# Where the sums of the first-layer weights are built, and in which form the second layer of the first sweep runs

## The chip, the core and the metric

The kernel runs on one core of a Trainium2 chip. The metric is the device time of one execution in microseconds (us), the median of several runs. Engines are named as in the profile: PE is TensorE (PEld its weight loads), DVE is VectorE, ACT is ScalarE, POOL is GpSimd, SP is SyncE, which in this kernel issues every DMA.

## What is computed

A causal, windowed attention (8 batches, 8 heads, 576 positions, head dimension 64, window 128, a linear bias by distance) gives 4608 tokens of 512 features. Two matrix products with a piecewise function between them follow. All is float32.

```python
rel = pos[:, None] - pos[None, :]
mask = (rel >= 0) & (rel < window)
scores = np.where(mask, scale * q @ k.T + bias, -1e9)
x = (softmax(scores) @ v)                      # 4608 x 512 after the heads are put side by side
h = x @ w_in                                   # 512 -> 2048
g = np.where(h >= 1, h, np.where(h <= -1, 0.0, (h + 1) ** 2 / 4))
out = g @ w_out                                # 2048 -> 512
```

## The kernel before

**Sweeps.** The 4608 tokens are cut into nine chunks of 512. Each chunk has a sweep (number c = 0 to 8) over the eight groups g of the feed-forward part; a group is two blocks of 128 of the 2048 hidden features, fc = g and fc = 8 + g. While the sweep of chunk c runs, the attention of chunk c + 1 is worked between its matmuls. What "first sweep" and "second sweep" mean below is c = 0 and c = 1.

**First layer.** In the first sweep a group is four plain products with the blocks A11, A12, A21, A22 of w_in (`plain`, L838 through `product`). From the second sweep on it is seven products with A11, A12, A22 and four sums of blocks, S1 to S4 (`prod`), in the manner of Strassen and Winograd. A float32 operand is kept as a high part of type float32r and a low part, the rest; a product is then three float32r matmuls of high and low parts. `build` makes such a pair out of a float32 block: a rounding copy (L506, through `rounded`, on ACT or DVE) and a subtraction on DVE (L507), and stores it to DRAM (L510). `operand` makes the sums first, with one DVE addition or subtraction each (L494). Later sweeps load the pairs from DRAM into a ring of ten tiles (`fetch`, L516). In the first sweep both the plain blocks and, once a group's A22 is asked for, its four sums are built.

**Weights.** They arrive as 64-bit numbers, so a block `raw` of 512 KB (L421) is turned into float32 by two passes of ACT (L451, L461) and two of DVE (L456, L464) in `convert`. A float32 first-layer group lies in one of three tiles (`w_of`).

**Second layer.** `layer2` adds the product of g's block with a block of w_out to four accumulators in PSUM, one per 128 tokens. Mostly both are high and low parts and there are three float32r matmuls (L879 to L881); `nonlinear` makes the parts of g (gh, L859, and gl, L861) and `split_out` those of w_out (L477, L478). In the first sweep groups 0 to 4 (`g < WHOLE`) do without: g and w_out stay float32 (tile `fo`), and one float32 matmul stands for the three (L872). For these groups `split_out` is called in the second sweep, where the parts are first needed.

**Slots.** `raw`, `fo` and the split w_out blocks `wo` share 17 slots of 4 KB per partition ("w" in pool "wp", NW = 17). 16 of them are in the end held by the 16 `wo`, for the rest of the kernel.

**Order.** `Plan` sets the order: every operation is recorded with its engine or engines, a cost, and what it reads and writes. A list scheduler with due times then lays them out (it may move a rounding copy, or the first step of `nonlinear`, from ACT to DVE or back), and the instructions are emitted in that order. On the chip each engine runs its own list strictly in that order.

Of the kernel before, what the change touches and what calls it, by code (L numbers as in the profile page):

```python
# [56 lines left out]
class Plan:  # L57
# [22 lines left out]
    def op(self, alts, reads=(), writes=()):  # L80

        node = Node(alts, set())
        reads = [x if isinstance(x, tuple) else (x, None) for x in reads]
        writes = [x if isinstance(x, tuple) else (x, None) for x in writes]

        def touched(table, key):
            return [n for k, v in table.items() if key is None or k is None or k == key for n in v]

        for b, key in reads + writes:
            assert not b.over, b.name  # L90
            if b.before is not None:
                b.before.over = True
            node.deps.update(touched(b.writers, key))
        for b, key in writes:
            node.deps.update(touched(b.readers, key))
            if not touched(b.writers, key) and b.before is not None:
                node.deps.update(b.before.nodes)
        for b, key in writes:
            if key is None:
                b.writers, b.readers = {}, {}  # L100
            b.writers[key] = [node]
            b.readers.pop(key, None)
        for b, key in reads:
# [191 lines left out]
def windowed_attention_then_ffn(  # L295
# [26 lines left out]
    LIGHT = 2  # L322
    FIRST = 1
    WHOLE = 5
# [99 lines left out]
    def convert(i):  # L424
# [6 lines left out]
        elif g < WHOLE:  # L431
            if f == 0:
                fo[g] = plan.shared(pools["wp"], "w", NW, [P, 2, DM], F32, f"fo_{g}", lambda free: True)
                kept.append((g, fo[g]))
            w, key = fo[g], f
# [30 lines left out]
    def split_out(g, f):  # L466

        o, key = (fo[g], f) if g < WHOLE else (fo.pop((g, f)), None)
        w = wo_of[f * NG + g] = plan.shared(pools["wp"], "w", NW, [P, 2, DM], F32R, f"wo_{g}_{f}", lambda free: (
            g >= WHOLE or all(x.slot is not None for _, x in kept)))  # L470
        if g >= WHOLE:
            kept.append((g, w))

        def whole():
            return o.t if key is None else o.t[:, key]

        plan.op(rounded(DM, lambda: w.t[:, 0], whole), [(o, key)], [(w, 0)])  # L477
        plan.op(dve(DM, lambda: V.tensor_tensor(w.t[:, 1], whole(), w.t[:, 0].bitcast(F32), ALU.subtract), True),  # L478
                [(o, key), (w, 0)], [(w, 1)])

    scratch, sums_w = {}, {}
# [17 lines left out]
    def build(g, name):  # L499
        b, key, f = operand(g, name)  # L500
        if name in PLAIN:
            t = buf("ring", "r", 10, [P, 2, 2, P], F32R, f"b_{g}_{name}")
        else:
            i = SUMS.index(name)
            t = buf(*(("ap", f"kk{i}", 1) if i < 2 else ("fp", "o", 2)), [P, 2, 2, P], F32R, f"b_{g}_{name}")
# [19 lines left out]
    def load_qk(p):  # L525
# [14 lines left out]
        if c < LIGHT:  # L540
# [10 lines left out]
    def load_v(p):  # L551
# [7 lines left out]
        if c < LIGHT and p % 2:  # L559
# [8 lines left out]
    def prepare_q(p):  # L568
# [5 lines left out]
        elif c < LIGHT:  # L574
# [4 lines left out]
        for j in range(2):  # L579
            if c < LIGHT:  # L580
# [54 lines left out]
    def scores(m, blks):  # L635
# [34 lines left out]
        if c < LIGHT:  # L670
# [26 lines left out]
    def weights_t(m):  # L697
# [13 lines left out]
        if c < LIGHT:  # L711
# [36 lines left out]
    def values(m):  # L748
# [32 lines left out]
        if c < LIGHT:  # L781
# [63 lines left out]
    def nonlinear(c, fc, h, src, f):  # L845
# [18 lines left out]
    def layer2(c, n, fc, t):  # L864
# [5 lines left out]
        if c == 0 and fc % NG < WHOLE:  # L870
            w, g, key = fo[fc % NG], gs[c, fc], fc // NG
            plan.op(pe(0.861, lambda: T.matmul(a.t, g.t[:, ts], w.t[:, key], start=first, stop=False)), [g, (w, key)], [a])  # L872
# [24 lines left out]
    for m in range(NH):  # L897
# [6 lines left out]
        if j and p + 1 < NH // 2:  # L904
# [20 lines left out]
    def weights_upto(n):  # L925
        while converted[0] < min(n, len(WEIGHTS)):
# [4 lines left out]
            if second_matrix and g >= WHOLE:  # L931
# [8 lines left out]
    def operands_upto(n):  # L940
        while asked[0] < min(n, len(todo_w)):
# [19 lines left out]
    def sweep_steps(c):  # L961
        steps = []
        for g in range(NG):
# [36 lines left out]
            def plain(i, tt, st=st, g=g):  # L1000
# [24 lines left out]
            if c == 1 and g < WHOLE:  # L1025
                steps[-1].append(lambda g=g: (split_out(g, 0), split_out(g, 1)))
# [68 lines left out]
```

## Time and profile before

| | |
|---|---|
| runs before | 993.31, 993.52, 994.74 us; median 993.52 us |
| the profiled execution | 994.51 us, of which its span on the core is 992.7 us |
| granted clock of PE | 1.00 in the whole span |
| first sweep's feed-forward (first to last group's start of the next sweep) | about 41 to 161 us |
| second sweep | 161.15 to 267.7 us |
| third sweep | 267.7 to 373.3 us |
| HBM | 176.82 MB read, 26.21 MB written |

A row of a group of instructions reads: line, engine, operation, out<-in by the program's names, shapes, count | busy us, mean ns of one | idle time of the engine ahead of them and what ended it. The busy time of an engine is the union of its instructions' records; two DVE or ACT instructions that follow each other at once overlap in the record by nearly 0.1 us, so the step from start to start is shorter than the mean of one. A row of a wait reads: who waited for whom: us in all, times, longest. A row of windows reads: the stretch, its length, then the busy time of PE, PEld, DVE, ACT, POOL with the count of instructions, the granted clock, the DMA engines' busy share, GB/s.

### The profile page before, as it was taken

Reading aid. Unit: us, or ns where it says so; the run is one execution under the profiler, and the core shown is the slowest. Engines: PE = TensorE matmul, PEld = TensorE weight load, DVE = VectorE, ACT = ScalarE, POOL = GpSimd, SP = SyncE. Lnnn points to the kernel's source line nnn. Section 1 sums busy time; section 2 is a strip of 40 time slices with the busy share of each in tenths; the row PEclk is TensorE's granted clock in tenths of the full one; section 3 lists DMA queues with packets and bytes.
Section 4 is the critical chain, followed back from the end, with each engine's and each line's share of the span. In section 5 each row is a group of like instructions: output and inputs, shape, how many; then the busy total and the mean of one; then the engine's idle time right before and its main releaser. Section 6 shows DMA issues by size and latency. Waiting matters only on the chain.

```text
span 992.7 us, 19604 instructions
## 1 busy us (share of the span) xinstructions
PE 983.4 (99%) x6456; PEld 886.2 (89%) x6456; DVE 813.5 (82%) x2118; ACT 654.5 (66%) x1619; POOL 195.5 (20%) x274
## 2 busy tenths in 40 slices
PE   9999999999999999999999999999999999999998
PEld 8887779989989999999999999999999999998987
DVE  7899999997887789777987798878877897885453
ACT  7997767966776568666775577667765676654222
POOL 3310201221231114111321122112311131210000
PEclk9999999999999999999999999999999999999999
DMA  9778885766676666766576658665766677456651
GB/s 347 296 237 289 301 299 168 243 185 197 177 227 189 188 191 204 222 181 198 174 239 200 189 165 260 185 182 179 244 187 186 188 202 222 154 159 193 188 157 43
DMA packets 104532, 204.33 MB, mean 206 GB/s; under 512 B 12400, under 2 KB 12400, under 8 KB 104432
## 3 DMA queue, kind: packets, MB, share of 16 engines
q1 hardware_dynamic: 104432, 203.08, 66.6%
q8 instruction: 53, 0.87, 0.4%
q14 instruction: 47, 0.39, 0.1%
HBM read 176.82 MB, written 26.21 MB: 205 GB/s over the span
## 4 chain that ended last, share of the span: by engine, by line
PE 92%; ACT 4%; DVE 2%; DMA 1%; issue 1%; POOL 0%; ACTq 0%; DVEq 0%; POOLq 0%
PE hA L838 17%; PE hB L838 13%; PE acc L879 12%; PE acc L880 12%; PE acc L881 12%; PE x L775 8%; PE h L838 5%; PE acc L872 3%; PE p L708 3%; PE s L668 3%; PE s L667 2%; ACT z L681 1%; PE s L665 1%; DMA out_dram<-o 1%; PE idle L1032 0%
## 5 line engine op out<-in xcount | busy, mean ns | idle before, releaser
L879 PE MATMUL acc<-wo,gh 128*128 128x512 f32 x536 | 216.5, 404 | 0.0
L880 PE MATMUL acc<-wo,gh 128*128 128x512 f32 x536 | 211.8, 395 | 0.0
L881 PE MATMUL acc<-wo,gl 128*128 128x512 f32 x536 | 210.1, 392 | 0.0
L739 POOL TENSOR_SCALAR_AFFINE_SELECT lu<-lu 128x512 fp32r<-128x512 f32 x112 | 92.9, 829 | 568.7 <-ACT lu L732 551.7
L982 ACT COPY s<-hA 128x256 f32<-128x256 f32 x192 | 70.7, 368 | 97.8 <-PE hA L838 96.9
L977 DVE TENSOR_TENSOR h<-hB,s 128x256 f32<-128x256 f32 x192 | 80.8, 421 | 54.0 <-PE hB L838 31.3
L681 ACT ACTIVATE z<-z,nmax 128x128 f32<-128x128 f32 x288 | 112.7, 393 | 16.9 <-DVE nmax L677 16.2
L881 PEld LDWEIGHTS acc<-wo,gl 128*128 128x128 f32 x536 | 100.7, 188 | 22.8
L838 PEld LDWEIGHTS hA<-x_T,w_S 128*128 128x128 f32 x768 | 107.3, 189 | 9.8 <-ACT s L982 0.4
L838 PE MATMUL hA<-x_T,w_S 128*128 128x256 f32 x768 | 111.9, 281 | 0.0
L879 PEld LDWEIGHTS acc<-wo,gh 128*128 128x128 f32 x536 | 101.7, 190 | 8.3
L880 PEld LDWEIGHTS acc<-wo,gh 128*128 128x128 f32 x536 | 101.8, 190 | 7.6
L852 ACT ACTIVATE m<-m 128x512 f32<-128x512 f32 x144 | 90.5, 628 | 21.6 <-DVE m L849 19.8
L854 DVE SCALAR_TENSOR_TENSOR h<-h,m 128x512 f32<-128x512 f32 x128 | 88.4, 691 | 9.8 <-ACT m L852 9.5
L861 DVE TENSOR_TENSOR gl<-h,gh 128x512 fp32r<-128x512 f32 x128 | 88.3, 690 | 2.6 <-ACT gh L359 0.7
L674 DVE COPY_PREDICATED s<-older,s 128x256 f32<-128x256 uint32 x144 | 60.6, 424 | 24.7 <-PE s L668 17.9
L742 POOL TENSOR_SCALAR_AFFINE_SELECT lu<-lu 128x512 fp32r<-128x512 f32 x112 | 75.4, 696 | 0.0
L775 PEld LDWEIGHTS x<-lu,vs 128*128 128x128 f32 x560 | 71.2, 190 | 2.6 <-POOL lu L742 0.5
L677 DVE CUSTOM_DVE_ANT_0 z<-s,rel 128x128 f32<-128x128 f32 x288 | 70.9, 285 | 1.6
L775 PE MATMUL x<-lu,vs 128*128 128x256 f32 (+1 forms) x560 | 71.3, 274 | 0.1
L849 DVE TENSOR_SCALAR m<-h 128x512 f32<-128x512 f32 x86 | 38.8, 451 | 37.8 <-ACT h L988 35.1
L988 ACT COPY h<-hA 128x256 f32<-128x256 f32 x64 | 23.8, 371 | 66.5 <-PE hA L838 65.6
(119 smaller groups left out, 2106.7 us busy)
## 6 DMA issues: line engine op xcount, KB each, us to landing
w_S<-d_S SPq DMA_DIRECT2D x256, 256.0 KB, 2.8
w_A<-d_A SPq DMA_DIRECT2D x192, 256.0 KB, 2.9
kr<-in_k_dram SPq DMA_DIRECT2D x112, 160.0 KB, 3.2
vn<-in_v_dram SPq DMA_DIRECT2D x33, 320.0 KB, 3.7
out_dram<-o SPq DMA_DIRECT2D x36, 256.0 KB, 3.9
qr<-in_q_dram SPq DMA_DIRECT2D x33, 256.0 KB, 3.2
raw<-in_moe_w_in_dram SPq DMA_DIRECT2D x16, 512.0 KB, 5.7
raw<-in_moe_w_out_dram SPq DMA_DIRECT2D x16, 512.0 KB, 6.9
```

The lines of the kernel that those rows point to most:

```text
L681: plan.op({"ACT": (0.385, 0.48, lambda i=i: S.activation(z.t[:, i], z.t[:, i], AF.Exp, bias=nmax.t[:, i:i + 1], scale=-1.0, accum_out=sm.t ...
L739: G.affine_select(out=lu[s].t[:, 0:2 * nb:2], in_=a.bitcast(F32), pattern=[[0, nb], [-1, P]], base=0, channel_multiplier=1, compare_op=ALU ...
L742: G.affine_select(out=a, in_=a.bitcast(F32), pattern=[[0, nb], [1, P]], base=0, channel_multiplier=-1, compare_op=ALU.is_ge, fill=0.0)
L775: T.matmul(px[:, q0 * P:q1 * P], sv, mv.rearrange("p a w -> p (a w)"), start=(w == 0), stop=(w == len(todo) - 1), skip_group_check=True)
L838: T.matmul(o.t[:, at:at + 2 * P], w.t[:, a, kb], x.t[:, b, kb], start=start and n == 0, stop=stop and n == len(todo) - 1, skip_group_check ...
L852: plan.op(act_fn(n, lambda: S.activation(m.t, m.t, AF.Square, scale=0.5)), [m], [m])
L854: plan.op(dve(n, lambda: V.scalar_tensor_tensor(f.t, h.t, 1.0, m.t, ALU.max, ALU.min), not psum), src + [m], dst)
L861: plan.op(dve(n, lambda: V.tensor_tensor(gl.t, f.t, gh.t.bitcast(F32), ALU.subtract), True), dst + [gh], [gl])
L879: T.matmul(a.t, gh.t[:, ts], w.t[:, 0], start=first, stop=False)
L880: T.matmul(a.t, gh.t[:, ts], w.t[:, 1], start=False, stop=False)
L881: T.matmul(a.t, gl.t[:, ts], w.t[:, 0], start=False, stop=last)
L977: plan.op(dve(2 * P, lambda: V.tensor_tensor(f.t[:, key * 2 * P:(key + 1) * 2 * P], b.t[:, :2 * P], s.t, ALU.add)), [b, s], [(f, key)])
```

## The change

1. `WHOLE` goes. In the first sweep every group has g and w_out in high and low parts and three float32r matmuls; `split_out` runs for all sixteen blocks in the first sweep, and the float32 matmul of L872 goes.
2. `LATE = 6`: for groups 2 to 7 the sums S1 to S4 are no longer built in the first sweep. `spill` stores the group's float32 first-layer weights to DRAM (two DMAs of 256 KB), `unspill` loads them in the second sweep (one of 512 KB) into one of the 17 shared slots, and only once all sixteen `wo` have their slot. The sums are then built in the second sweep, straight into the ring tiles that the products read, and stored from there for the third and later sweeps. The second sweep fetches no sums for these groups.
3. `LIGHT` counts pairs of heads instead of chunks: 8 pairs are the 2 chunks of before, so the same branches are taken.

```diff
-    LIGHT = 2
+    LIGHT = 8
-    WHOLE = 5
+    LATE = 6
...
     def split_out(g, f):
-        o, key = (fo[g], f) if g < WHOLE else (fo.pop((g, f)), None)
-        w = wo_of[f * NG + g] = plan.shared(pools["wp"], "w", NW, [P, 2, DM], F32R, f"wo_{g}_{f}", lambda free: (
-            g >= WHOLE or all(x.slot is not None for _, x in kept)))
...
+        o = fo.pop((g, f))
+        w = wo_of[f * NG + g] = plan.shared(pools["wp"], "w", NW, [P, 2, DM], F32R, f"wo_{g}_{f}", lambda free: True)
+        kept.append((g, w))
...
+    def spill(g):
+        d = spilled[g] = plan.buf(dr, f"d_w_{g}", 1, [P, 2, DM], F32, f"d_w_{g}")
+        for f in range(2):
+            plan.op(dma(P * DM * 4, lambda f=f, w=w_of[g]: DMA.dma_start(d.t[:, f], w.t[:, f])), [(w_of[g], f)], [(d, f)])
+
+    def unspill(g):
+        w = w_of[g] = plan.shared(pools["wp"], "w", NW, [P, 2, DM], F32, f"w32_{g}", lambda free: (
+            all(x.slot is not None for _, x in kept)))
+        d = spilled.pop(g)
+        plan.op(dma(P * DM * 8, lambda: DMA.dma_start(w.t, d.t)), [d], [w])
...
     def build(g, name):
         b, key, f = operand(g, name)
-        if name in PLAIN:
+        if name in PLAIN or g >= NG - LATE:
             t = buf("ring", "r", 10, [P, 2, 2, P], F32R, f"b_{g}_{name}")
...
-        if c == 0 and fc % NG < WHOLE:
-            gs[c, fc] = f
-            return
...
-        if c == 0 and fc % NG < WHOLE:
-            w, g, key = fo[fc % NG], gs[c, fc], fc // NG
-            plan.op(pe(0.861, lambda: T.matmul(a.t, g.t[:, ts], w.t[:, key], start=first, stop=False)), [g, (w, key)], [a])
...
-            have[c, g, x] = fetch(c, g, x) if c else build(g, x)
+            late = g >= NG - LATE
+            if late and c == 1 and x == "A11":
+                unspill(g)
+            made = c == 0 or late and c == 1 and x in SUMS
+            have[c, g, x] = build(g, x) if made else fetch(c, g, x)
             if c == 0 and x == "A22":
-                for name in SUMS:
-                    build(g, name)
+                if late:
+                    spill(g)
+                else:
+                    for name in SUMS:
+                        build(g, name)
```

The order that the scheduler makes of it, at three places. First DVE in the first sweep, around the last step of the piecewise function for the first block of group 1 (g_0_1: the numbers in that name are the chunk and the block; in w, b, S and wo the first is the group). Before:

```order
L464 ISA fo_0_767<-raw_3_344,fo_0_767 128x1024
L686 RECIPROCAL rc_11_922<-rc_11_922 128x4
L507 TENSOR_TENSOR b_2_A11_915<-w_2_891,b_2_A11_915 128x256
L692 TENSOR_TENSOR z_11_851<-z_11_851,rc_11_922 128x512
L507 TENSOR_TENSOR b_2_A12_917<-w_2_891,b_2_A12_917 128x256
L456 TENSOR_SCALAR w_2_891<-raw_9_474 128x512
L456 TENSOR_SCALAR fo_1_952<-raw_6_408 128x512
L854 SCALAR_TENSOR_TENSOR g_0_1_954<-h0_0_1_838,m_0_1_925 128x512
L464 ISA w_2_891<-raw_9_474,w_2_891 128x1024
L494 TENSOR_TENSOR S1_0_966<-w_0_433 128x256
```

Now:

```order
L469 TENSOR_TENSOR wo_0_1_985<-fo_0_1_939,wo_0_1_985 128x512
L362 CAST b_2_A12_1003<-w_2_972 128x256
L497 TENSOR_TENSOR S2_1_1006<-S1_1_896,w_1_727 128x256
L687 TENSOR_SCALAR rc_11_1008<-sum_11_955 128x4
L497 TENSOR_TENSOR S3_1_1011<-w_1_727 128x256
L688 RECIPROCAL rc_11_1008<-rc_11_1008 128x4
L856 SCALAR_TENSOR_TENSOR g_0_1_1020<-h0_0_1_847,m_0_1_957 128x512
L694 TENSOR_TENSOR z_11_941<-z_11_941,rc_11_1008 128x512
L509 TENSOR_TENSOR b_2_A11_995<-w_2_972,b_2_A11_995 128x256
L509 TENSOR_TENSOR b_1_S2_1022<-S2_1_1006,b_1_S2_1022 128x256
```

Before, the first sum of group 0 (S1_0) stood behind this step; now all sums of group 0 and most of group 1, and the split of both w_out blocks of group 0 (wo_0_1), stand ahead of it or right beside it.

Second, DVE in the second sweep, late in group 5, where the low parts kl of the next keys, the sums xn of the attention's output and gl are made. Before:

```order
L609 TENSOR_TENSOR kl_12_3327<-kr1_12_3068,kk1_12_3334 128x640
L592 SCALAR_TENSOR_TENSOR ql_12_3320<-qr_12_3084,ql_12_3320 64x512
L861 TENSOR_TENSOR gl_1_13_3425<-h1_1_5_3284,gh_1_13_3409 128x512
L789 TENSOR_TENSOR xn_2_2316<-x_22_3392,xn_2_2316 64x512
L733 TENSOR_TENSOR lu1_23_3448<-p_23_3429,lu0_23_3440 128x4x128
L977 TENSOR_TENSOR h1_1_6_3462<-hB_1_6_3352,s4_1_6_3454 128x256
```

Now (w32_6 and w32_7 are the weights of groups 6 and 7 that came back from DRAM):

```order
L497 TENSOR_TENSOR S4_6_3472<-w32_6_3304,S2_6_3380 128x256
L611 TENSOR_TENSOR kl_12_3476<-kr0_12_3094,kk0_12_3219 128x640
L594 SCALAR_TENSOR_TENSOR ql_12_3410<-qr_12_3266,ql_12_3410 64x512
L509 TENSOR_TENSOR b_6_S4_3478<-S4_6_3472,b_6_S4_3478 128x256
L856 SCALAR_TENSOR_TENSOR h1_1_5_3347<-h1_1_5_3347,m_1_13_3433 128x512
L791 TENSOR_TENSOR xn_2_2326<-x_22_3460,xn_2_2326 64x512
L611 TENSOR_TENSOR kl_12_3476<-kr1_12_3130,kk1_12_3445 128x640
L860 TENSOR_TENSOR gl_1_13_3522<-h1_1_5_3347,gh_1_13_3511 128x512
L735 TENSOR_TENSOR lu1_23_3533<-p_23_3500,lu0_23_3514 128x4x128
L497 TENSOR_TENSOR S1_7_3540<-w32_7_3480 128x256
```

Between the last reader of w32_6 (S4_6) and the first reader of w32_7 (S1_7) there are eight DVE instructions; the two tiles share the one slot that the sixteen `wo` leave.

Third, SP in the second sweep. Before, the loads of group 3's operands and the inputs of the attention:

```order
L516 DMA w_1_3_S2_2604<-d_3_S2_1474 128x512
L566 DMA vn_10_2624<-in_v_dram 128x640
L516 DMA w_1_3_S3_2636<-d_3_S3_1508 128x512
L516 DMA w_1_3_S1_2646<-d_3_S1_1351 128x512
L548 DMA kr0_11_2655<-in_k_dram 64x640 x2
L516 DMA w_1_3_S4_2687<-d_3_S4_1549 128x512
L516 DMA w_1_3_A22_2707<-d_3_A22_1178 128x512
L548 DMA kr1_11_2717<-in_k_dram 64x640 x2
```

Now:

```order
L512 DMA d_2_S3_2613<-b_2_S3_2576 128x512
L484 DMA w32_3_2637<-d_w_3_1209 128x1024
L550 DMA kr0_11_2669<-in_k_dram 64x640 x2
L512 DMA d_2_S4_2705<-b_2_S4_2647 128x512
L518 DMA w_1_3_A22_2712<-d_3_A22_1307 128x512
L518 DMA w_1_4_A11_2751<-d_4_A11_1387 128x512
L512 DMA d_3_S2_2762<-b_3_S2_2742 128x512
L512 DMA d_3_S3_2778<-b_3_S3_2749 128x512
```

The four loads of sums have gone, and stores of sums (d_2_S3 and so on) and the load of w32_3, which wait for DVE, stand in the same queue ahead of the loads of A22 and A11.

More of the change, by code (lines that the diff above doesn't have):

```diff
@@ L107, in op @@
                 node.need = b
+            elif b.tag:
+                assert b.nodes[0] in node.deps or any(b.nodes[0] in d.deps or d is b.nodes[-1] for d in node.deps), b.name
             if node not in b.nodes[-1:]:
@@ L430, in convert @@
             w, key = w_of[g], f
[L431 to L435, printed above, removed]
         else:
@@ L466, in split_out @@
     def split_out(g, f):
-        o, key = (fo[g], f) if g < WHOLE else (fo.pop((g, f)), None)
-        w = wo_of[f * NG + g] = plan.shared(pools["wp"], "w", NW, [P, 2, DM], F32R, f"wo_{g}_{f}", lambda free: (
-            g >= WHOLE or all(x.slot is not None for _, x in kept)))
[L471 to L481, printed above, removed]
+        o = fo.pop((g, f))
+        w = wo_of[f * NG + g] = plan.shared(pools["wp"], "w", NW, [P, 2, DM], F32R, f"wo_{g}_{f}", lambda free: True)
+        kept.append((g, w))
+        plan.op(rounded(DM, lambda: w.t[:, 0], lambda: o.t), [o], [(w, 0)])
+        plan.op(dve(DM, lambda: V.tensor_tensor(w.t[:, 1], o.t, w.t[:, 0].bitcast(F32), ALU.subtract), True),
+                [o, (w, 0)], [(w, 1)])
+    scratch, sums_w, spilled = {}, {}, {}
+    def spill(g):
[7 more added lines that the diff above has]
+        plan.op(dma(P * DM * 8, lambda: DMA.dma_start(w.t, d.t)), [d], [w])
     def operand(g, name):
@@ L500, in build @@
         b, key, f = operand(g, name)
-        if name in PLAIN:
+        if name in PLAIN or g >= NG - LATE:
             t = buf("ring", "r", 10, [P, 2, 2, P], F32R, f"b_{g}_{name}")
         else:
-            i = SUMS.index(name)
-            t = buf(*(("ap", f"kk{i}", 1) if i < 2 else ("fp", "o", 2)), [P, 2, 2, P], F32R, f"b_{g}_{name}")
+            t = buf("fp", "o", 2, [P, 2, 2, P], F32R, f"b_{g}_{name}")
         plan.op(rounded(2 * P, lambda: t.t[:, 0], f), [(b, key)], [(t, 0)])
@@ L558, in load_v @@
             return
-        if c < LIGHT and p % 2:
+        if p < LIGHT and p % 2:
             t = buf("ap", "vs", 1, [P, 2, 5, P], F32, f"vn_{p}")
@@ L599, in prepare_k @@
         c = p // NPAIR
-        if c < LIGHT:
+        if p < LIGHT:
             return
@@ L613, in prepare_v @@
         c = p // NPAIR
-        if c < LIGHT:
+        if p < LIGHT:
             return
@@ L907, in windowed_attention_then_ffn @@
             work.append((m, 4, m, [lambda p=p: prepare_k(p + 1)]))
-            early = NPAIR <= p + 2 < NH // 2 and p + 2 != LIGHT * NPAIR
+            early = NPAIR <= p + 2 < NH // 2 and p + 2 != LIGHT
             work.append((m, 5, m, [lambda p=p: prepare_q(p + 1)] + ([lambda p=p: load_qk(p + 2)] if early else [])))
-            if p + 1 == LIGHT * NPAIR:
+            if p + 1 == LIGHT:
                 work.append((m, 3.5, m, [lambda p=p: load_qk(p + 1)]))
@@ L930, in weights_upto @@
             converted[0] += 1
-            if second_matrix and g >= WHOLE:
+            if second_matrix:
                 split_out(g, f)
@@ L1009, in plain @@
                 if tt:
-                    tag = ("gh", 4) if g < WHOLE else ("h", 3)
-                    nonlinear(c, i * NG + g, h, [h], buf("fp", *tag, [P, 4 * P], F32, f"g_{c}_{i * NG + g}"))
+                    nonlinear(c, i * NG + g, h, [h], buf("fp", "h", 3, [P, 4 * P], F32, f"g_{c}_{i * NG + g}"))
             if c == 0:
@@ L1024, in sweep_steps @@
                     steps += [[second]] * fill
-            if c == 1 and g < WHOLE:
-                steps[-1].append(lambda g=g: (split_out(g, 0), split_out(g, 1)))
             pend = [lambda g=g, i=i, t=t: layer2(c, 2 * g + i, i * NG + g, t) for i in range(2) for t in range(SIZES[c])]
```

21 lines of the change are left out of this document (9 added, 12 removed).

## The prediction

> **What bounds the kernel now.** I read the totals first, then the chain of work that ended last, then what PE waited for, then the busy times by sweep.
>
> ```profile
> PE 983.4 (99%) x6456; PEld 886.2 (89%) x6456; DVE 813.5 (82%) x2118; ACT 654.5 (66%) x1619; POOL 195.5 (20%) x274
> PE 92%; ACT 4%; DVE 2%; DMA 1%; issue 1%; POOL 0%; ACTq 0%; DVEq 0%; POOLq 0%
> ```
>
> PE is busy nearly all the time and is 92% of the chain. What it waited for in the whole span:
>
> ```profile
> PE idle L1032 <- POOL qscale L385: 1.7, 1, 1.7
> PE s L665 <- ACT lu L721: 1.5, 1, 1.5
> PE p L708 <- DVE z L692: 1.0, 1, 1.0
> PE hB L838 <- DVE h L977: 0.7, 2, 0.5
> PE p L708 <- DVE rc L685: 0.5, 1, 0.5
> PE hB L838 <- DVE g L854: 0.2, 1, 0.2
> ```
>
> That is 5.6 us in all, 4.7 of it in the first 41 us. So PE's own work sets the time, and a saving of PE work is a saving of time as long as the other engines can follow. Whether they can is read by stretch (start-up in three pieces, rest of the first sweep, second sweep, third sweep):
>
> ```profile
> 10.00:41.10 31.10, 28.15 (x200) 25.66 (x199) 27.65 (x118) 30.79 (x101) 12.82 (x18) 1.00 0.96 374
> 41.10:66.80 25.70, 25.70 (x190) 23.36 (x189) 23.33 (x70) 25.38 (x60) 3.29 (x5) 1.00 0.67 224
> 66.80:161.15 94.35, 94.29 (x551) 74.20 (x550) 89.91 (x246) 71.02 (x170) 11.73 (x11) 1.00 0.81 274
> 161.15:267.70 106.55, 106.02 (x706) 96.15 (x705) 96.55 (x240) 76.41 (x187) 25.22 (x33) 1.00 0.66 200
> 267.70:373.30 105.60, 105.09 (x705) 96.29 (x704) 87.14 (x226) 70.27 (x175) 23.29 (x32) 1.00 0.67 197
> ```
>
> The third number is DVE, the fourth ACT. ACT has no idle time up to 66.8 us (0.3 of 31.1 and 0.3 of 25.7). DVE is idle for 2.4 and 4.4 us in the first sweep after 41.1 us, 6.8 us of 120, and for 10.0 us of the second sweep; from the third sweep on it has 18.5 us to spare. So the change takes PE work out of the one sweep in which DVE is nearly as full as PE, and puts DVE work into the next fullest.
>
> **PE: float32 matmuls out.** A float32 matmul stands in the records as two passes; the chain shows the pair's time, and the start times of three float32r matmuls in mid-kernel show theirs.
>
> ```profile
> L872 PE MATMUL acc<-fo,g 128*128 128x512 f32 x80 | 39.1, 592 | 0.0
> 57.85 0.86 PE acc L872 x2
> 600.45 0.40 PE L879 MATMUL acc<-wo,gh 128*128 128x512 f32 x1
> 600.68 0.40 PE L880 MATMUL acc<-wo,gh 128*128 128x512 f32 x1
> 600.92 0.39 PE L881 MATMUL acc<-wo,gl 128*128 128x512 f32 x1
> 601.15 0.87 PE L838 MATMUL hA<-x_T,w_S 128*128 128x256 f32 x6
> ```
>
> 80 records are 40 float32 matmuls (5 groups x 2 blocks x 4 token tiles) of 0.86 us. Three float32r ones take 601.15 - 600.45 = 0.70 us. So PE loses 40 x (0.86 - 0.70) = 6.4 to 6.5 us of work, all in the first sweep. Nothing else on PE changes: the same counts of products and attention matmuls, the same last instructions at the end of the kernel. I take **-6.5 us**.
>
> **DVE and ACT in the first sweep.** The step prices of DVE, from start to start where it runs without a gap:
>
> ```profile
> 142.66 0.42 DVE L507 TENSOR_TENSOR b_A<-w,b_A 128x256 fp32r<-128x256 f32 x1
> 143.00 0.42 DVE L494 TENSOR_TENSOR S<-S,w 128x256 f32<-128x256 f32 x1
> 143.33 0.69 DVE L854 SCALAR_TENSOR_TENSOR g<-h,m 128x512 f32<-128x512 f32 x1
> 143.94 0.42 DVE L456 TENSOR_SCALAR fo<-raw 128x512 int32<-128x512 int32 x1
> 144.27 0.42 DVE L507 TENSOR_TENSOR b_A<-w,b_A 128x256 fp32r<-128x256 f32 x1
> 145.27 0.69 DVE L464 CUSTOM_DVE_ANT_0 fo<-raw,fo 128x1024 uint16<-128x1024 uint16 x1
> 145.88 0.43 DVE L674 COPY_PREDICATED s<-older,s 128x256 f32<-128x256 uint32 x1
> ```
>
> A two-input step of 256 columns takes 0.34 or 0.33 us, one of 512 columns 0.61, a copy or one-input step of 512 from SBUF 0.33, the second step of a weight's conversion 0.61. Up to the first addition of the second sweep (h0_1_0) DVE's list has lost 24 sums and 24 subtractions of b_S (48 x 0.335 = 16.1). It has gained 10 subtractions gl and 12 of wo (22 x 0.61 = 13.4; before, 12 of the 16 wo were split after that point), two second steps and one first of the last w_out blocks (1.6), 9 rounding copies (3.0) and a few steps that the scheduler moved between DVE and ACT or to the other side of this point (4 ql and a step x_T more, 3 copies xn, 2 m, 1 z and two roundings fewer: about -1.4). Sum: **+0.5 us of DVE work while PE's shrinks by 6.5**. The idle time that DVE had to give was 6.8 us: 6.8 - 6.5 - 0.5 = -0.2. Even with no idle at all DVE would be a little late, and it is never without any for long.
>
> The squeeze is worst early, because the sums of groups 0 and 1, which stay in the first sweep, now stand further forward. Ahead of the step g_0_1 DVE has 7 sums and 5 subtractions b_S more (12 x 0.335 = 4.0), 2 wo and 1 gl (1.8), 9 roundings (six of them of half the width: 2.0) and 4 ql (1.3), and 3 z, 2 xn, 2 b_A and 2 conversion steps fewer (-4.4): +4.7 us. PE's list up to there is one product shorter (6 x 0.12) and has two float32 matmuls replaced (2 x 0.16): -1.0 us. So DVE wants 5.7 us, and was idle for 3.45 us between 10 and 41.1 us and 2.4 after: just enough, if not one gap is left. For ACT the prices are:
>
> ```profile
> L581 ACT ACTIVATE ql<-qr,qscale 128x512 f32<-128x512 f32 x6 | 4.3, 710 | 0.0
> L690 ACT ACTIVATE z<-z,rc 128x128 f32<-128x128 f32 x8 | 2.5, 392 | 0.0
> L359 ACT CAST b_A<-w 128x256 fp32r<-128x256 f32 x23 | 8.5, 398 | 2.7 <-DVE w L464 2.7
> L783 ACT COPY xn<-x 64x512 f32<-64x512 f32 x13 | 7.5, 576 | 0.3 <-PE x L775 0.2
> ```
>
> Less the overlap of nearly 0.1 us that follows from steps against means, and with like forms at like prices, its list up to the same point has 3 ql (1.9), 3 roundings b_A (0.9), 2 exponentials (0.6 at the least, as two of L690) and 1 copy (0.5) fewer, and 8 of L690 (2.4), 2 xn and 1 lu (1.5), 1 wo and 1 b_S (0.8) more: +0.8 us. ACT had 0.6 us idle in 57 us, so it wants 0.8 + 1.0 - 0.6 = 1.2 us more than there is. Both want their time at the same place, and these do not add; with something for idle time that cannot be filled I take a stall of PE of **+2.0 us** between 40 and 90 us. Its bounds: -0.5 (some of the 4.7 us of start-up waits goes with the new order) and +6.0 (DVE keeps the idle time that it has).
>
> **DVE in the second sweep.** It gains the 48 sum and b_S steps (+16.1) and some roundings (+0.4), and loses 12 wo (-7.3), the late conversions (-1.6) and 2 x_T (-1.2): +6.4 us against 10.0 us idle, 3.6 left. What uses it up: the loads of the weights into one slot. S4 of group g is the last reader; then SP issues the load of group g + 1, which must land before S1 of that group, and DVE stands still in its list if it has not. Between the two stand 8 to 12 DVE instructions; for groups 6 and 7, as the order shows, kl, ql, b_S, the step h, xn, kl, gl, lu, 0.7 + 0.7 + 0.34 + 0.61 + 0.61 + 0.7 + 0.61 + 0.61 = 4.9 us. The five gaps are 5.3, 4.0, 5.4, 4.0 and 4.9 us. Loads of the same size and row length are those of raw:
>
> ```profile
> L421 SPq DMA_DIRECT2D raw<-in_moe_w_in_dram x2: 424/436/448, 53.2 to 57.6; - x2
> DMA to landing us min/median/max: 4.0/4.1/5.5
> raw<-in_moe_w_out_dram SPq DMA_DIRECT2D x16, 512.0 KB, 6.9
> ```
>
> In the quiet stretch from 41 to 58 us they took 4.0 to 5.5 us (the last row, 6.9, is the median of the w_out loads, most of them in traffic of 0.8 DMA share and more). The second sweep stands between (0.66), nearer the first; with 0.2 us for the two hand-overs, 4.2 to 5.7 against the gaps gives a wait of 0 to 1.7 us in each of the two short gaps and near nothing in the others: 2 us in all, bounds 0 and, at 6.9, 11.9.
>
> By the fit in the Trainium skill's page "DMA: Bandwidth & Descriptors", section "Anatomy of one DMA — SWDGE (gpsimd) path", 2.0 us plus the bytes over 436 GB/s, such a load would take 3.2 us (an estimate from that page, whose fit is for another queue than SP's) and DVE would never wait. The quickest load of this trace, 4.0 us, does not agree, and the sum goes by the trace.
>
> The sums also move next to more POOL work: 25.22 us of the second sweep against 11.73 in most of the first. One sum shows what a select of POOL beside it costs:
>
> ```profile
> 86.05 0.66 DVE L494 TENSOR_TENSOR S<-w 128x256 f32<-128x256 f32 x1
> 86.50 0.71 POOL L727 TENSOR_SCALAR_AFFINE_SELECT lu<-lu 128x512 f32<-128x512 f32 x1
> 86.63 0.85 DVE L494 TENSOR_TENSOR S<-w,S 128x256 f32<-128x256 f32 x1
> L507 DVE TENSOR_TENSOR b_S<-S,b_S 128x256 fp32r<-128x256 f32 x32 | 13.6, 434 | 0.0
> ```
>
> The second sum took 0.85 us instead of 0.42. It is rare: b_S has a mean of 434 ns, so 32 of them lost 0.5 us together. Twice the POOL share makes this about 1 us for 48 steps. By the lock that the Trainium skill's page "SBUF — State Buffer", section "SBUF: two separate sides", states (a DVE step with two SBUF inputs and a POOL instruction that reads SBUF exclude each other for the whole instruction), every one of the 48 steps that starts beside a select, 24% of them, would wait for half of 0.7 us, 4 us in all; rows like 86.63 agree with the lock, the mean of 434 with a rarer one. So 3.6 - 2 - 1 = 0.6 us of idle time is left to DVE, which is too little not to be felt: **+0.5 us**, bounds -0.9 (the waits of hB in the list above go) and +8.
>
> SP: the second sweep issues 24 fetches fewer, 24 stores and 6 large loads more; they are 0.3 to 0.45 us of issue each in 106 us. The DMA share rises from 0.66 to about 0.7, the first sweep's falls. I cost it at nothing.
>
> **Sum.** -6.5 + 2.0 + 0.5 = -4.0 us. The profiled execution of 994.51 us becomes 990.5; the median of the runs is 1.0 us lower, 993.52, and becomes **989.5 us**. Its own range is 987.5 to 991.5.
>
> **Rivals.** *PE alone decides* (0.21): the scheduler's new order fills DVE and ACT better at the start, and the loads land in their gaps. For it: there is a stretch in which DVE has no gap and PE hardly waits.
>
> ```profile
> 140.00:160.00 20.00, 19.94 (x133) 17.58 (x132) 19.94 (x51) 15.55 (x35) 2.19 (x2) 1.00 0.69 227
> ```
>
> Time 993.5 - 6.5 = 987.0, and 986.1 if the hB waits go too.
>
> *DVE and ACT take it all* (0.17): DVE keeps its 6.8 us of idle time in the first sweep, because its in-order list waits for PE and ACT in turn.
>
> ```profile
> L977 DVE TENSOR_TENSOR h<-hB,s 128x256 f32<-128x256 f32 x192 | 80.8, 421 | 54.0 <-PE hB L838 31.3 <-ACT s L982 22.4
> ```
>
> For it: 54 us of its idle time stand ahead of this one addition. Against it: most of that lies in the later sweeps, which have room. PE then waits 6 us more: -6.5 + 6.0 + 0.5, about 993.5, between 991.5 and 994.5.
>
> *The one slot* (0.12), the other side: loads of 512 KB in the second sweep take 6.9 us as the median of w_out's did; DVE waits 1.8 + 3.1 + 1.7 + 3.1 + 2.2 = 11.9 us, and with DVE stand the stores and loads behind it on SP. 3.6 us of it is covered: -6.5 + 2.0 + 8.3 = +3.8, 997.3 us. It decides from a landing of about 6.1 us on, where the waits (7.9) exceed cover and saving (3.6 + 4.5). For it: 6.9 is measured; against it: that traffic was 0.8 to 1.0 of the DMA engines, here 0.66, where 4.1 is nearer.
>
> **Chances and range.** The forecast has 0.5. Over 0.2% of this time is 2 us, about what a measurement of this kernel tells from no change. Faster by more: the forecast, less a little of its upper end, and the first rival, 0.70. Within: the second rival and that end, 0.18. Slower: 0.12. The range from 986.3 to 993.0 holds the forecast, the first rival and most of the second.
>
> **What would show it.** Right: L872 gone; 120 matmuls more at L872 to L874's new lines at steps of 0.23; DVE without idle time from 41 to 100 us and PE waits for DVE or ACT of 1 to 3 us there; in the second sweep DVE waits for the DMA of w32 in two or three of five places, of 1 us each. Wrong: PE waits of over 4 us in the first sweep, a landing of w32 over 6 us, or PE waits for S tiles (b_S) in the second.

## The result and the profile after

The changed kernel takes 988.41 us (median of 6 runs, 987.15 to 989.43); the kernel before took 994.63 us beside it (993.31 to 996.44). The ratio is 0.9936, interval 0.9923 to 0.9949, a gain of 6.2 us. Forecast were 989.5 us and a gain of 4.0; the kernel before ran 1.1 us longer here than in the runs that the forecast started from. In its profiled execution (988.27 us, span 986.6) PE is busy for 5.7 us less, DVE for 5.5 us more; then the chain:

```profile
PE 977.7 (99%) x6496; PEld 894.1 (91%) x6496; DVE 819.0 (83%) x2137; ACT 653.4 (66%) x1623; POOL 187.6 (19%) x274
PE 91%; DVE 3%; ACT 3%; DMA 1%; issue 0%; SPq 0%; POOL 0%; POOLq 0%; ACTq 0%; DVEq 0%
```

What PE waited for in the changed kernel, in the whole span:

```profile
PE p L710 <- DVE z L694: 1.7, 3, 0.7
PE idle L1029 <- POOL qscale L387: 1.7, 1, 1.7
PE p L710 <- DVE nmax L679: 0.5, 1, 0.5
PE s L669 <- DVE lu L735: 0.4, 1, 0.4
PE h L840 <- DVE x_B L811: 0.3, 1, 0.3
PE s L667 <- ACT lu L723: 0.3, 1, 0.3
```

The waits for hB are gone; in their place stand many small waits, all but the one of 0.4 us in the first 70 us. By stretch, with the changed kernel's own sweep bounds from 57.5 us on:

```profile
10.00:41.10 31.10, 28.79 (x200) 25.17 (x199) 28.87 (x128) 29.90 (x101) 12.10 (x16) 1.00 0.89 347
41.10:57.50 16.40, 15.57 (x116) 14.27 (x115) 12.21 (x44) 16.30 (x42) 2.82 (x4) 1.00 0.63 197
57.50:157.50 100.00, 99.97 (x666) 91.68 (x665) 96.69 (x250) 81.84 (x186) 11.23 (x12) 1.00 0.79 271
157.50:262.90 105.40, 104.99 (x705) 96.32 (x704) 102.27 (x271) 77.04 (x196) 27.60 (x33) 1.00 0.69 216
262.90:367.80 104.90, 104.90 (x706) 96.25 (x706) 88.95 (x227) 70.66 (x177) 22.05 (x33) 1.00 0.68 204
```

ACT is nearly full up to 57.5 us (1.2 us idle of 31.1, then 0.1 of 16.4), DVE has 3.3 us idle in the 100 after that and 3.1 in the second sweep, and PE is hardly held up there (0.03 and 0.4 us idle). "Busy" hides part of a wait: a product's matmul has a record of 0.28 us and a step of 0.12, so a pause must exceed 0.16 us to show as idle. Sweeps are therefore compared from start to start. The first matmul of hA of a sweep is its first product; for the second sweep it is the first start in these rows (kernel before, then changed):

```profile
L838 PE MATMUL hA<-x_B,w_A x384: 274/282/332, 161.2 to 967.4; 128*128 128x256 f32 x192
```

```profile
L840 PE MATMUL hA<-x_B,w_A x384: 274/283/333, 157.5 to 961.2; 128*128 128x256 f32 x192
```

The same starts in all profiled executions give this table, in us (the last column ends with the start of PE's last matmul; the names of the experiments follow below):

| kernel | up to the second sweep | second sweep | third | the rest |
|---|---|---|---|---|
| before | 161.15 | 106.55 | 105.64 | 615.36 |
| changed | 157.52 | 105.42 | 104.81 | 614.75 |
| after_again | 158.01 | 105.72 | 104.86 | 614.76 |
| late0 | 168.56 | 105.51 | 104.65 | 614.89 |
| halfB | 160.53 | 107.26 | 104.88 | 615.36 |
| kk | 154.57 | 105.80 | 104.93 | 615.36 |
| kk_again | 155.06 | 105.79 | 104.93 | 615.36 |
| kk0 | 162.60 | 114.11 | 104.97 | 615.98 |
| kk4 | 156.04 | 109.78 | 104.88 | 615.37 |
| kk5 | 154.30 | 108.71 | 105.27 | 615.36 |
| kk7 | 155.02 | 106.35 | 105.82 | 615.36 |
| late8 | 154.07 | 108.83 | 108.61 | 615.36 |
| twice | 157.49 | 117.70 | 105.26 | 614.76 |
| once_half | 157.37 | 116.38 | 105.32 | 614.76 |

In every sweep PE's matmuls are the same in kind and number in all these kernels but kk0, save the second-layer ones of the first sweep; what differs beyond those are pauses and the matmuls' own steps. So the 6.2 us are 3.6 in the first sweep (PE's 6.5 less a loss of 2.9), 1.1 in the second, 0.8 in the third and 0.6 in the rest. The loss is all early: at the first matmul of h0_0_1 (56.79 us before, 57.52 now) PE is 0.7 us later with 2.2 us less work behind it.

The loads of the stored weights (L484), and when they land:

```profile
L484 SPq DMA_DIRECT2D w<-d_w x6: 319/320/358, 152.9 to 241.5; - x6
DMA to landing us min/median/max: 3.4/3.9/5.2
```

In the changed kernel's list of waits DVE never waits for them. The gaps from S4 to the next S1 were 5.3, 4.6, 5.4, 4.4 and 5.0 us. The five loads landed 0.0, 0.6, 1.6, 1.0 and 0.8 us ahead of S1: the first of them landed at 190.95 us, and S1 began at 190.97.

### The profile page after: what moved, and what is told of

Read it like the earlier page. It is cut to its first block, busy times and chain, and to the rows that moved or that the text cites. A ratio compares the mean times of both kernels' runs of the same rounds, so it can differ in the third digit from the quotient of the medians.

```text
span 986.6 us, 19652 instructions
## 1 busy us (share of the span) xinstructions
PE 977.7 (99%) x6496; PEld 894.1 (91%) x6496; DVE 819.0 (83%) x2137; ACT 653.4 (66%) x1623; POOL 187.6 (19%) x274
## 4 chain that ended last, share of the span: by engine, by line
PE 91%; DVE 3%; ACT 3%; DMA 1%; issue 0%; SPq 0%; POOL 0%; POOLq 0%; ACTq 0%; DVEq 0%
PE hA L840 19%; PE hB L840 14%; PE acc L872 13%; PE acc L873 13%; PE acc L874 13%; PE x L777 7%; PE h L840 3%; PE p L710 3%; PE s L669 3%; PE s L670 3%; PE s L667 1%; DMA raw<-in_moe_w_in_dram 1%; DMA raw<-in_moe_w_out_dram 1%; ACT z L683 1%; ACT raw L448 0%; ACT raw L458 0%
## 5 line engine op out<-in xcount | busy, mean ns | idle before, releaser
L872 PE MATMUL acc<-wo,gh 128*128 128x512 f32 x576 | 232.9, 404 | 0.0
L873 PE MATMUL acc<-wo,gh 128*128 128x512 f32 x576 | 227.5, 395 | 0.0
L874 PE MATMUL acc<-wo,gl 128*128 128x512 f32 x576 | 225.6, 392 | 0.0
L741 POOL TENSOR_SCALAR_AFFINE_SELECT lu<-lu 128x512 fp32r<-128x512 f32 x112 | 80.4, 718 | 573.5 <-ACT lu L734 556.2
L874 PEld LDWEIGHTS acc<-wo,gl 128*128 128x128 f32 x576 | 108.4, 188 | 24.7
L872 PEld LDWEIGHTS acc<-wo,gh 128*128 128x128 f32 x576 | 109.2, 190 | 9.1
L873 PEld LDWEIGHTS acc<-wo,gh 128*128 128x128 f32 x576 | 109.5, 190 | 8.2
L840 PEld LDWEIGHTS hA<-x_T,w_S 128*128 128x128 f32 x696 | 97.8, 190 | 8.3
L840 PE MATMUL hA<-x_T,w_S 128*128 128x256 f32 x696 | 101.8, 283 | 0.0
L744 POOL TENSOR_SCALAR_AFFINE_SELECT lu<-lu 128x512 fp32r<-128x512 f32 x112 | 81.5, 751 | 0.0
L851 DVE TENSOR_SCALAR m<-h 128x512 f32<-128x512 f32 x100 | 45.1, 451 | 33.9 <-ACT h L988 31.5
```

Of the source, the lines that this page charges most:

```text
L741: G.affine_select(out=lu[s].t[:, 0:2 * nb:2], in_=a.bitcast(F32), pattern=[[0, nb], [-1, P]], base=0, channel_multiplier=1, compare_op=ALU ...
L744: G.affine_select(out=a, in_=a.bitcast(F32), pattern=[[0, nb], [1, P]], base=0, channel_multiplier=-1, compare_op=ALU.is_ge, fill=0.0)
L840: T.matmul(o.t[:, at:at + 2 * P], w.t[:, a, kb], x.t[:, b, kb], start=start and n == 0, stop=stop and n == len(todo) - 1, skip_group_check ...
L872: T.matmul(a.t, gh.t[:, ts], w.t[:, 0], start=first, stop=False)
L873: T.matmul(a.t, gh.t[:, ts], w.t[:, 1], start=False, stop=False)
L874: T.matmul(a.t, gl.t[:, ts], w.t[:, 0], start=False, stop=last)
```

## The experiments

My theory: DVE and ACT are as full as PE in the first sweep, so the shorter PE work is worth its 6.5 us only with the sums out of that sweep, and the move alone is worth nothing. The main rival: PE alone decides.

**late0: the second layer alone.**

```diff
-    LATE = 6
+    LATE = 0
```

> The changed kernel with LATE = 0: the sums of all groups are made in the first sweep as before, and only the second-layer part of the change is left (3 float32r matmuls for the 40 in float32). It holds TensorE's 6.5 us saving whole, and nothing of the second sweep changes. Theory (VectorE and ScalarE must have room in the first sweep, and the later sums give it): VectorE owes 10.3 us more than it has at the first matmul of g_0_0, and 63.6 us of work stand ahead of g_0_1 (54.9 in the changed kernel), so TensorE waits some 9 to 12 us more in the first 60 us: 997 to 1001 us, ratio to the kernel before 1.003 to 1.007. Rival (TensorE's own work alone decides): as the changed kernel, 987 to 989 us, ratio 0.993 to 0.994.

Measured: 1000.05 us beside 994.99; ratio 1.0053, interval 1.0040 to 1.0066. Slower than before, with the 6.5 us of PE work gone: the rival is dead. PE's waits between 30 and 70 us:

```profile
PE p L710 <- DVE z L694: 4.5, 1, 4.5
PE x L777 <- issue: 2.2, 1, 2.2
PE h L840 <- DVE b_A L509: 1.7, 1, 1.7
PE h L840 <- DVE x_B L811: 1.1, 1, 1.1
PE s L667 <- ACT lu L723: 0.9, 1, 0.9
```

These are 10.4 us; in the changed kernel PE is idle for 2.1 us in the same stretch. Clock is lost with them: late0's trace shows a granted clock of 0.50 from 35.6 to 42.4 us and from 56.1 to 59.5. The table adds something unforeseen: with no sum moved, late0 has the changed kernel's short second and third sweeps (105.51 and 104.65).

**halfB: the sums alone.** The kernel before with `spill`, `unspill` and LATE; WHOLE = 5 and the float32 matmuls stay.

```diff
     WHOLE = 5
+    LATE = 6
...
-        if name in PLAIN:
+        if name in PLAIN or g >= NG - LATE:
...
+            late = g >= NG - LATE
+            if late and c == 1 and x == "A11":
+                unspill(g)
+            made = c == 0 or late and c == 1 and x in SUMS
```

> The kernel before with only the sums moved: sums of six groups in the second sweep from stored weights, the 40 float32 matmuls kept. Theory (the move brings TensorE no work less, it only makes room; the room is wanted when the float32 matmuls go): 992.5 to 994.6 us beside a kernel before of 994.6, ratio 0.998 to 1.000, the second and third sweeps shorter by the 1 to 2 us of waits that the changed kernel lost there. Rival (the move itself brings the gain, since VectorE and ScalarE are relieved in the first sweep): 4 to 6 us less than before, ratio 0.994 to 0.996.

Measured: 994.62 us; ratio 0.9993, interval 0.9985 to 1.0002. As the theory has it: no gain that can be measured. One part alone costs 5.1 us, the other brings 0.4, both together bring 6.2: the gain is neither part's but the two parts' together. The waits moved, too. halfB has one of 1.7 us near the end of the second sweep, while the kernel before had 0.7 in two places (the row shown in the prediction):

```profile
PE hA L851 <- ACT s L1002: 1.7, 1, 1.7
```

**kk: other buffers for the sums of groups 0 and 1.** The list of the change and the diff ahead of the prediction leave out one edit, this one in `build`:

```diff
-            i = SUMS.index(name)
-            t = buf(*(("ap", f"kk{i}", 1) if i < 2 else ("fp", "o", 2)), [P, 2, 2, P], F32R, f"b_{g}_{name}")
+            t = buf("fp", "o", 2, [P, 2, 2, P], F32R, f"b_{g}_{name}")
```

Before, S1 and S2 had the buffers kk0 and kk1. In the changed kernel all four sums of groups 0 and 1 go through the two buffers ("fp", "o"), and so do all float32 w_out blocks (before, those of groups 0 to 4 had shared slots); the sums must be done before the next blocks can be converted. kk puts the four sums into kk0 and kk1 in turn. These two are not free for the whole sweep: they hold the high parts of the attention's keys (`prepare_k`), in kk from 128 us on.

```diff
-            t = buf("fp", "o", 2, [P, 2, 2, P], F32R, f"b_{g}_{name}")
+            t = buf("ap", f"kk{SUMS.index(name) % 2}", 1, [P, 2, 2, P], F32R, f"b_{g}_{name}")
```

> The changed kernel with the sums of groups 0 and 1 in a buffer each (the tags kk0 and kk1) and not in the two rotating buffers that the float32 blocks of the second weights use as well; so the sums need not be done before the blocks of the next group are split: 47.7 us of VectorE's work stand ahead of g_0_1 for 54.9. Theory (the 2.7 us that the changed kernel loses before 57 us come from the sums being forced forward through these buffers): the loss goes, 985 to 986.5 us, ratio 0.990 to 0.992. Rival (the loss is that of the start as such, with two groups' weights to come in and to be split): as the changed kernel, 987.7 to 989.1 us, ratio 0.993 to 0.9945.

Measured: 986.77 us; ratio 0.9918, interval 0.9904 to 0.9931. The early loss is gone: h0_0_1 starts at 54.72 us, 2.8 earlier, and the second sweep 2.95 earlier. The first places at which PE waited in the kernel before are back, with nearly their old sizes:

```profile
PE s L667 <- ACT lu L723: 1.5, 1, 1.5
PE p L710 <- DVE z L694: 1.0, 1, 1.0
PE x L777 <- DVE nmax L679: 0.6, 1, 0.6
PE p L710 <- DVE rc L687: 0.5, 1, 0.5
```

Of the 2.95 us, 1.1 are given back later (0.5 in the second and third sweeps, 0.6 in the rest).

**twice and once_half: the loads made late.** The load of the stored weights is issued twice, or followed by its second half once more, into the same buffer; in the traces the second goes out when the first has landed.

```diff
-        plan.op(dma(P * DM * 8, lambda: DMA.dma_start(w.t, d.t)), [d], [w])
+        plan.op(dma(P * DM * 8, lambda: [DMA.dma_start(w.t, d.t) for _ in range(2)]), [d], [w])
```

```diff
-        plan.op(dma(P * DM * 8, lambda: DMA.dma_start(w.t, d.t)), [d], [w])
+        plan.op(dma(P * DM * 8, lambda: [DMA.dma_start(w.t, d.t), DMA.dma_start(w.t[:, 1], d.t[:, 1])]), [d], [w])
```

> The changed kernel with each load of stored float32 weights in the second sweep issued twice, the second into the same buffer after the first, so that the weights are ready after 7.5 to 8 us for 3.9. VectorE's gaps ahead of the first sum of a group are 4.4 to 5.4 us, so it waits some 2.5 to 3.5 us at each of five groups, 13 to 16 us in all. Price by the prediction's rival of the one slot (TensorE waits as soon as the load is later than the gap): 8 to 13 us more than the changed kernel, ratio 1.001 to 1.007. Rival (the sums are made far enough ahead of TensorE that the waits go into its cover): 0 to 3 us more, ratio 0.9935 to 0.997.

> The changed kernel with half of each load of stored float32 weights issued once more behind it, so the weights are ready after some 5.5 to 6 us for 3.9 (7 to 7.5 with the whole load twice). VectorE's gaps ahead of the first sum are 4.4 to 5.4 us: it waits 0.3 to 1.5 us at each of five groups, 2 to 6 us in all. With the load twice VectorE waited 14.4 us and the time rose by 13. Theory (the first 1 to 1.5 us of each wait lie in the lead of the sums, and the clock falls only after longer ones): 988.4 to 990 us, ratio 0.993 to 0.995. Rival (each us of wait is a us of time, from the first on): 990.5 to 994.5 us, ratio 0.9955 to 0.9995.

Measured: twice 1001.33 us, ratio 1.0065 (1.0052 to 1.0079); once_half 998.86 us, ratio 1.0033 (1.0020 to 1.0045). Twice is 12.9 us over the changed kernel, within the 8 to 13 expected by the price of the rival "the one slot". For once_half both expectations missed, as the dose was not the half: from the first issue to S1 it took 6.6 to 7.9 us (twice 6.7 to 8.5). DVE's wait in twice, then in once_half:

```profile
DVE S L497 <- DMA w<-d_w: 14.4, 5, 3.2
```

```profile
DVE S L497 <- DMA w<-d_w: 12.0, 5, 3.2
```

The second sweep grew by 12.3 and by 11.0 us against the changed kernel: nearly a us of time for a us of wait. PE's waits in it, once_half:

```profile
PE hA L840 <- ACT s L982: 4.0, 2, 2.4
PE hB L840 <- DVE h L977: 3.4, 4, 1.2
PE s L669 <- DVE lu L735: 0.6, 1, 0.6
PE p L710 <- DVE z L694: 0.2, 1, 0.2
```

That is 8.2 us, 0.4 of which the changed kernel has too; so some 4 us of DVE's 12 were covered, near the 3.6 of the prediction, and about 3 us came on top. Part of them is PE's clock (two-us windows of once_half; in this view PE alone is shown, and the clock follows it):

```profile
196.00:198.00 2.00, 0.84 (x5) 0.91 0.35 130
198.00:200.00 2.00, 2.00 (x9) 0.50 0.76 276
200.00:202.00 2.00, 2.00 (x12) 0.73 0.83 269
202.00:204.00 2.00, 2.00 (x19) 1.00 0.49 143
```

After a wait of 1.67 us the granted clock is 0.50 for some 3.4 us, which costs about 1.7.

**kk0, kk4, kk5, kk7, late8: how many groups to move.** kk with LATE = 0, 4, 5 and 7; late8 is the changed kernel with LATE = 8, which leaves no sum in those buffers.

```diff
-    LATE = 6
+    LATE = 4
```

> No sums moved (LATE = 0) and the 40 float32 matmuls gone, as in late0, but the first two sums of each group in buffers of their own (kk0, kk1), as the kernel before has them. It tells the sums' work from the shared buffers in late0's 1000.0 us. Counted along the order, VectorE has 59.9 us of work ahead of g_0_1 (late0 63.6, the changed kernel with these buffers 47.7, the kernel before 49.3) and 74.4 ahead of g_0_2 (74.6, 61.2, 60.0). Theory (work, not buffers: the sums of six groups are 12 to 13 us that don't fit into the start): VectorE is 6 to 7 us behind TensorE, so 992 to 996 us, ratio 0.997 to 1.001, and the move of the sums is worth 5 to 9 us. Rival (late0 paid for the shared buffers): 986 to 988.5 us, ratio 0.991 to 0.9935, and the move was not needed.

> The changed kernel with buffers of their own for the first two sums, and the sums of four groups moved for six. VectorE's lead over TensorE counted along the order is at its lowest 6.1 us (6.4 with six groups moved, 2.4 to 0.2 in the changed kernel), and two groups' loads and sums leave the second sweep. Theory (a lead of 6 us in the first sweep is enough, and the second sweep hides its sums): as kk, 986.2 to 987.4 us, ratio 0.991 to 0.993. Rival (each group moved pays by itself): 2 us or more above kk, 988.8 us or more, ratio over 0.9935.

> The changed kernel with the sums of all eight groups moved. The start is then as in kk (no sum in the first sweep), and the second sweep has loads and sums at groups 0 and 1 as well: VectorE's work there is some 106 us of a sweep of 105.4. Theory (VectorE's room in the second sweep, 2 to 3 us as measured in the changed kernel, ends here, but the sums lie ahead of their matmuls by some 5 us): 986.5 to 989 us, ratio 0.9915 to 0.994. Rival (loads in one slot at every group decide in the second sweep): 990 us or more, ratio 0.995 or more.

> As kk (sums of the groups that stay in the first sweep in buffers of their own), with the sums of five groups moved for six. Theory, as the four-group run left it (VectorE is full from 60 us on in the first sweep, so each group whose sums stay there costs its VectorE work: 4.8 us for two groups, 11 us for the next four): kk + 2 to 3 us, 988.5 to 990 us, ratio 0.9935 to 0.995. Rival (the four-group run paid only for the reuse of the two buffers, which begins with the fourth group's sums): kk + 0 to 1 us, 986.3 to 987.8 us, ratio 0.991 to 0.993.

> As kk, with the sums of seven groups moved for six. Theory (in the second sweep VectorE is full as well with six groups, and eight cost 8.8 us more there than six; the first sweep has nothing left to give, its losses after 60 us being 0.6 us in kk): kk + 1 to 5 us, 988 to 992 us, ratio 0.993 to 0.997. Rival (only the group 0 that follows on the sweep's first products is too early for its load): as kk or better, 985.5 to 987.5 us, ratio 0.990 to 0.9925.

| groups moved | 0 (kk0) | 4 (kk4) | 5 (kk5) | 6 (kk) | 7 (kk7) | 8 (late8) |
|---|---|---|---|---|---|---|
| median us | 1002.74 | 991.57 | 991.52 | 986.77 | 988.23 | 995.60 |
| ratio to before | 1.0078 | 0.9965 | 0.9967 | 0.9918 | 0.9938 | 1.0008 |
| interval | 1.0065-1.0091 | 0.9952-0.9977 | 0.9957-0.9977 | 0.9904-0.9931 | 0.9925-0.9951 | 0.9994-1.0022 |

kk0 was no faster than late0 and 7 us slower than even the theory had it, but it does not tell work from buffers cleanly. Its first sweep is 6.0 us shorter than late0's, so there the shared buffers counted; it is still 8.0 us longer than kk's, which has the same buffers and the sums of six groups less. Its second sweep is 8.6 us longer than late0's: with the sums of all groups in kk0 and kk1 the first copy of keys into them starts at 164.1 us (late0 108.3, kk 128.1), and one of these copies waits for the store of a sum; some attention matmuls of the first sweep come in the second, and PE's granted clock is 0.50 for 6.8 us from 178 us on. kk7 came out as the theory expected, late8 on its rival's side, and kk5 above both. Four groups were expected to do as well as six, and I was wrong. DVE's lead, counted along the order, leaves out the time in which DVE itself stands still; no run shows that this is the whole reason. PE's waits at the turn to the second sweep (150 to 180 us), kk4:

```profile
PE hA L840 <- ACT s L982: 1.5, 2, 1.0
PE acc L874 <- DVE gl L860: 0.8, 1, 0.8
PE hB L840 <- DVE g L856: 0.5, 1, 0.5
```

In that stretch DVE is busy all but 0.5 us in kk4 and all but 0.3 in kk:

```profile
150.00:180.00 30.00, 27.26 (x173) 23.53 (x173) 29.51 (x68) 22.80 (x54) 7.64 (x8) 1.00 0.70 222
```

```profile
150.00:180.00 30.00, 29.73 (x197) 26.75 (x196) 29.70 (x69) 22.82 (x54) 8.95 (x11) 1.00 0.59 180
```

So DVE is as full there in both, and PE gets less done in kk4: I read this as work that the sums of the two more groups pushed back, which no run shows by itself. By the times the price is no even one for each group: 2.8 us each from none to four (with kk0's loss to the keys in it), nothing from four to five, 4.7 for the sixth. kk5's profiled execution (989.48 us) is its quickest, so its trace shows only part of that step; why it is so steep stays open. Beyond six the second sweep pays, where DVE is busy for 29.8 of 30 us already (kk, 180 to 210 us): late8's second and third sweeps are 6.7 us longer than kk's. PE's waits in late8 from 150 to 300 us:

```profile
PE hB L840 <- DVE h L977: 1.6, 2, 1.3
PE acc L874 <- DVE gl L860: 0.7, 1, 0.7
PE s L669 <- DVE lu L735: 0.6, 1, 0.6
PE s L669 <- DVE ql L594: 0.4, 1, 0.4
```

late8's times scatter from 992.59 to 999.88 us, and the profile is of the lowest.

**kk_again and after_again: the two best side by side.** The kernel of kk and the changed kernel, unaltered, on one chip.

> The kernel of kk once more, on one chip with the changed kernel itself, to compare the two directly: 986.5 to 987.5 us, 1 to 2 us under the changed kernel. If the 1.6 us between them came from the sessions: equal within 0.7 us.

> The changed kernel, unaltered, on one chip with kk: 988 to 989 us, ratio 0.993 to 0.9945, 1 to 2 us over kk. If the difference came from the sessions: equal within 0.7 us.

Measured: 986.91 us (0.9926, 0.9912 to 0.9940) and 988.02 us (0.9939, 0.9926 to 0.9952). kk is 1.1 us ahead here and was 1.6 ahead across sessions; the intervals overlap. kk is the quickest kernel of this study in both places, by 0.1 to 0.2%.

## Why the prediction was right, and where it was not

- *What bounds the kernel: PE, as long as the others can follow.* Right, and the condition is the whole case: late0 has the shorter PE work and is slower than before.
- *PE: -6.5 us.* Nothing measured speaks against it. PE has 40 matmul records more (120 for 80); at h0_0_1 and at the second sweep the loss comes out the same, 2.9 us, with 2.2 and with 6.5 us of PE work saved.
- *First sweep: +2.0, bounds -0.5 and +6.0.* The size was near (2.9; 3.4 in after_again), the place only in part: the first of the new waits stands at 13 us, and from 57.5 us on PE loses nothing, where 40 to 90 was said. Between 41 and 57.5 us PE is idle for 0.8 us (before, none), ACT for 0.1 and DVE for 4.2: ACT was as short of time as I had it, DVE was not. I counted the sums that "stand further forward" and did not ask why the order puts them there: two buffers shared with the w_out blocks, by an edit that my list of the change leaves out. kk shows that the loss hangs on these buffers.
- *Second sweep: +0.5.* This step failed, in sign: -1.1, then -0.8 in the third sweep and -0.6 in the rest, where the sum had nothing. Two causes. The loads landed after 3.9 us, not 4.2 to 5.7, and the short gaps were 4.6 and 4.4, not 4.0, so DVE waited for none; DVE's work itself (102.3 us against 96.55 + 6.4 = 103.0) was foretold. And the waits of hB went, which I had priced at -0.9 as a bound, without seeing that the longest lies in the third sweep. late0 lost them in these two sweeps as well with no sum moved, so the move did not do that. For the third sweep the traces point to a cause, though no run varies it. late0 has there the very order of the kernel before on PE, DVE and ACT, and is 1.0 us shorter. ACT's copy of an output tile (`o`, two buffers) waits until an earlier store to DRAM has landed; behind it on ACT stands a copy of h, for which DVE waits, and PE's hB waits for DVE (the copy and the wait of hB in the kernel before, then the copy in late0):

```profile
292.71 0.59 ACT L886 COPY o<-acc 128x512 f32<-128x512 f32 x1 [2.42 <-DMA out_dram<-o]
296.25 0.98 PE L838 MATMUL hB<-x_B,w_A 128*128 128x256 f32 x6 [0.51 <-DVE h L977]
297.08 0.59 ACT L879 COPY o<-acc 128x512 f32<-128x512 f32 x1 [0.46 <-DMA out_dram<-o]
```

The store took 6.1 us in the kernel before, 4.1 in late0 and 2.9 in the changed kernel, where the copy does not wait; and the kernel before itself needs 0.8 us less for its fourth sweep, with the same order on PE. late0 shows the same in its fourth sweep: the copy waits 2.21 us, hB 0.3, and that sweep is 0.6 us longer than its fifth. So the gain in the third sweep seems to be mostly that of one store that landed sooner, which nothing in the change aims at. What took away the smaller waits of the second sweep no run tells.

- *SP at nothing.* No row speaks against it.
- *Sum.* -4.0 forecast, -6.2 measured: the time fell into the range through an early loss 0.9 us larger than thought and later sweeps 3.0 us better, and that is luck. Of the signs named for "right" only the first came, the 120 matmuls at steps of 0.23 in place of L872's: DVE was idle for 4.6 us between 41 and 100 us, PE for 0.9, and DVE waited for no load of w32. Of the signs named for "wrong" none came (PE is idle for 3.2 us between 10 us and the second sweep, no load took over 5.2, and PE waited for no b_S). That it is near the 6.5 of the rival "PE alone decides" is chance: late0 and halfB contradict that rival's mechanism.
- *The one slot.* Its mechanism is real and its price near (twice, once_half), and the kernel is close to it: one load landed 0.02 us ahead of its S1, in kk one of 4.9 us made DVE wait for 0.5, and in halfB the same loads took 5.6 to 6.5 us in the second sweep, where longer gaps (7 us and more) hid them. The Trainium skill's page "DMA: Bandwidth & Descriptors" (section "Anatomy of one DMA — SWDGE (gpsimd) path"), whose fit gave an estimate of 3.2 us, named the right side; the quickest load here took 3.4, the median 3.9.

## What to carry to other kernels

When the bounding engine is relieved in a stretch in which another engine is as full, the gain must be bought by moving that engine's work elsewhere; test each half alone, since here each half alone was worth nothing or less. How much to move had an optimum here, six groups of eight, at which the stretch that receives the work is full as well. When a change moves work through a rotating buffer, look at what else uses that buffer: it sets the order as surely as a dependence does.

## What the runs showed of the hardware

- The granted clock of PE fell to 0.50, for 3.4 or 6.8 us at a time, around waits that were not long: 1.67 us in once_half, 1.68 in twice (0.44 us of idle shortly ahead of it), 1.18 in kk0 (0.52 ahead of it), besides 4.47 in late0 and 3.49 in kk0; but not around 1.71 us in halfB, 2.38 in once_half and 2.89 in twice. The length of one wait therefore does not tell. A matmul of 512 columns then steps by 0.43 us for 0.23. The Trainium skill's page "TensorE: Matmul & The Clock Gate" (section "HAM oscillation — how this bites in real kernels") advises to have no PE idle gaps over about 3.4 us; here half of that was too much in once_half, and 2.89 was not in twice.
- Half the bytes took four fifths of the time: the five loads of 256 KB that DVE waited for in once_half landed after 2.6 to 3.3 us (mean 2.9), the five of 512 KB in their place in twice after 3.2 to 3.9 (mean 3.5). DVE's wait shrank only from 14.4 to 12.0 us.
- From the fourth sweep on, kernels whose sums share the w_out buffers took 614.75 to 614.89 us, those with kk0 and kk1 (and late8) 615.36, and kk0 615.98 (it and late0 have a wait of some 0.3 us at 406 us in it), though PE's work is the same. The order is not the reason: late0 has kk's order on PE, DVE and ACT there. No run shows what is.
